# A fused attention and ResMLP kernel: LN1's beta as three PE rows, q by head groups and first-batch buffers in hT

## The chip, the cores and the metric

The kernel runs on one core of one Trainium2 chip. The metric is device microseconds (us) of a run. PE is the matmul engine, DVE the vector engine, ACT the scalar engine, and GpSimd (POOL in the views) is a further one; loads are issued by GpSimd, by SP and at the start by ACT. A transfer lands when all of its data has arrived; PE stands when it waits for something; the clock is the share of full speed that PE was granted. Most runs of a kernel agree within 0.3%. Medians are of 4 to 11 runs of the kernel before and 4 to 6 of the other. A ratio is the mean time of one kernel's fast runs over that of the other's of the same rounds, so it is not quite the ratio of the medians; it comes with a 95% interval.

## The reference, cut

```python
# q (8,16,384,64); k, v (8,4,384,64); four q heads share a k and v head
k = np.repeat(k, 4, axis=1); v = np.repeat(v, 4, axis=1)
scores = np.matmul(q, k.transpose(0, 1, 3, 2)) / np.sqrt(64)
attn = softmax(scores); attn_out = np.matmul(attn, v)
x = attn_out.transpose(0, 2, 1, 3).reshape(8, 384, 1024)
a1 = alpha1 * x + beta1                       # "LN1"
u = x + lam * np.einsum('ts,bsd->btd', w_tok, a1)   # token mix over 384 tokens
a2 = alpha2 * u + beta2
out = u + lam * (np.maximum(a2 @ w_ch1, 0.0) @ w_ch2)   # 1024 -> 4096 -> 1024
```

All tensors are f32 in HBM; the kernel computes in bf16 with f32 sums.

## The kernel before

For each of eight batches there is a side job (`side`: attention, token mix and transposes that end in `a2T`) and a main job (`main`: the MLP; the h matmuls with w1, then the ch matmuls with w2). The side job of batch b+1 is woven into the main job of batch b, and PE is full there. Only batch 0's side job stands alone, in front of everything: **the first stage**. The w1 matrix is streamed anew for every batch through a ring of five chunks (512 KB each as bf16), w2 is loaded once. GpSimd issues those loads, as it issues all loads that cast f32 to bf16.

The parts that the change touches, with cuts marked (`...`):

```python
            if hh == 0:
                avs[p] = psum.tile([P, 2, NST, D1], f32, tag="mm" if first else "av", name="av",
                                   bufs=2 if first else 1)
            av = avs[p]
            hk = (2 * p + hh) // G
            for sq in range(NST):
                for sk in range(NST):
                    k = (p * NST + sk) * NST + sq
                    nc.tensor.matmul(out=av[:, hh, sq, :], lhsT=ess[k // 4][:, hh, k % 4, :],
                                     rhs=vb[:, sk, hk, :], start=(sk == 0), stop=(sk == NST - 1))
            if hh == 0:
                if first and p in (0, 2):
                    r = slice(0, 256) if p == 0 else slice(256, DM)
                    nc.vector.tensor_tensor(out=g1[:, r], in0=g1[:, r], in1=lam_t[:, r], op=MUL)
                    nc.vector.tensor_tensor(out=h1[:, r], in0=h1[:, r], in1=lam_t[:, r], op=MUL)
                return
            rinv = sb.tile([P, 2, NST, 1], f32, tag="rinv", name="rinv", bufs=1)
            nc.vector.reciprocal(out=rinv, in_=av[:, :, :, D:])
            for hh in range(2):
                c0 = (2 * p + hh) * D
                nc.vector.tensor_tensor(out=x[:, :, c0:c0 + D], in0=av[:, hh, :, :D],
                                        in1=rinv[:, hh].to_broadcast([P, NST, D]), op=MUL)
            t = sb.tile([P, NST, P], f32, tag="tmp", name="a1f", bufs=4)
            nc.vector.tensor_tensor(out=t, in0=x[:, :, cols(p)], in1=bc(g1, p), op=MUL)
            a1s[p] = sb.tile([P, NST, P], bf, tag="a1", name="a1", bufs=2)
            eng = nc.gpsimd if first and p < NP - 2 else nc.vector
            eng.tensor_tensor(out=a1s[p], in0=t, in1=bc(h1, p), op=ADD)
        ...
        def tok(p):
            ps = psum.tile([P, NST, P], f32, tag="av" if first else "sc", name="tok",
                           bufs=1 if first else 2)
            for tt in range(NST):
                for st in range(NST):
                    nc.tensor.matmul(out=ps[:, tt, :], lhsT=wtokT[:, st, tt * P:(tt + 1) * P],
                                     rhs=a1s[p][:, st, :], start=(st == 0), stop=(st == NST - 1))
            u = x[:, :, cols(p)]
            nc.vector.tensor_tensor(out=u, in0=ps, in1=u, op=ADD)
            a2s[p] = sb.tile([P, NST, P], bf, tag="a2", name="a2", bufs=3)
            nc.vector.tensor_tensor(out=a2s[p], in0=u, in1=bc(al2, p), op=MUL)

        def a2_transpose(p):
            if not pe_flip or first and p < NP - 3:
                nc.sync.dma_start_transpose(
                    out=a2T[:, p, :S].rearrange("p (a s) -> p a s", a=NST),
                    in_=a2s[p].rearrange("p a d -> p (a d)"))
```

The prologue, in the order in which each engine meets its instructions, and the loads woven into the first stage (the key is the index of a step of `side(0)`):

```python
        nc.scalar.dma_start(out=qst, in_=q[0, :G].rearrange("h (p st) d -> p h st d", st=NST))
        load_q(0, [0], G)
        ...
        nc.gpsimd.tensor_copy(out=vt[0][:, :, :, :D], in_=vst.rearrange("p h st d -> p st h d"))
        place_k(0, 0)
        for h, cp in ((0, nc.vector.tensor_copy), (2, nc.scalar.copy)):
            cp(out=qrs[0][:, :, h:h + 2, :], in_=qst[:, h:h + 2].rearrange("p h st d -> p st h d"))
        load_k(1)
        for t, ap in ((g1, moe_alpha1), (lam_t, moe_lam), (h1, moe_beta1)):
            bcast(nc.scalar, t, ap, 0, 256)
            bcast(nc.sync, t, ap, 256, DM)
        bcast(nc.sync, al2, moe_alpha2, 0, DM)
        wtok_in = stage[:, 1, :NST * S // 2].bitcast(bf).rearrange("p (tt s) -> p tt s", tt=NST)
        ...
        for c in range(RING):
            load_w1(c)
        loads = {7: [(load_w2, 0, 0, 2)], 25: [(load_q, 1, [0]), (load_q, 1, [1])],
                 31: [(load_q, 1, [2]), (load_v, 1, [0])], 37: [(load_v, 1, [1])], 43: [(load_v, 1, [2])]}
        for i, f in enumerate(side(0)):
            f()
            for g, *a in loads.get(i, []):
                g(*a)
            if i == 4:
                place_k(0, 1)
```

In `main(0)` each chunk's end issues the chunk five further on, and for most chunks a piece of w2 as well. The first step of `side(1)` that needs q of batch 1 is its second, a transpose on PE, which comes after 32 h matmuls.

The softmax here doesn't subtract the row's maximum and nothing guards it: scores larger than these inputs give would overflow.

## Time and profile before

| | before |
|---|---|
| median of runs | 830.34 us (4 runs) |
| span of the profiled run | 828.8 us |
| first stage (to the first h matmul) | 52.04 us |
| a steady batch | 97 us, PE busy 96.40 |
| GpSimd's first w1 load | 8.67 us |
| last part of batch 1's q lands / PE wants it | 55.1 / 59.28 us |

The prediction below shows the lines that carry it. The two rows are the DMA view of the first 60 us in 40 slices of 1.5 us (busy share in tenths, then GB/s): the 16 DMA engines are busy from 3 to 57 us.

```profile
DMA  0599999999999999999999999899999999999208
GB/s 0 136 324 321 164 191 229 139 200 188 198 197 197 228 322 325 308 358 213 189 196 202 206 200 151 135 198 195 197 186 178 122 149 138 157 140 230 61 4 96
```

The view of waits between 20 and 52 us: who waited for what (total, times, longest). The same figure stood in a view that I had asked for before I predicted (waits from 0 to 52 us), but I did not weigh it, and it matters later: the DVE stood for the a2 buffer 1.0 us, although the chain of waits shows a DMA piece of 8.32.

```profile
DVE a L247 <- DMA a2T<-a: 1.0, 1, 1.0
```

### The profile page before, as it was taken

The page shows a single profiled execution, that of the slowest core. Times are in us where ns is not written, and L with a number is a line of the kernel's source. Part 1 is how long each engine was busy: PE and PEld are TensorE (multiplying, and loading weights), DVE is VectorE, ACT ScalarE, POOL GpSimd, SP SyncE. Part 2 cuts the span into 40 slices and gives each one's busy share as a digit, 9 for nine tenths or more (in the row PEclk, how much of TensorE's full clock was granted, in tenths as well). Part 3 has the DMA queues.
Part 4 walks back from the last instruction along what each step waited for, and adds up shares of the span by engine and source line. Part 5 has one row for each costly group of instructions (what it writes and reads, how often), then busy time and mean ns, then how long its engine had stood idle before and what let it go on. Part 6 is the DMA issues. An engine that isn't in the chain of part 4 may idle for free.

```text
span 828.8 us, 13904 instructions
## 1 busy us (share of the span) xinstructions
PE 797.1 (96%) x5958; PEld 445.9 (54%) x6011; DVE 350.9 (42%) x728; ACT 219.0 (26%) x287; POOL 187.6 (23%) x229
## 2 busy tenths in 40 slices
PE   5679999999999999999999999999999999999997
PEld 2456555566455654556555664556545565556543
DVE  3854645234452445434443344434444344442222
ACT  3514331233103321043211332133310342102100
POOL 5414441033302250022400224012410221003000
PEclk7869999999999999999999999999999999999999
DMA  9999999799948999499917999379995999119701
GB/s 193 230 145 181 200 210 190 138 175 151 140 97 134 176 169 90 97 166 173 169 46 138 181 169 138 82 128 179 174 91 111 130 176 141 37 55 182 97 38 39
DMA packets 265342, 115.09 MB, mean 139 GB/s; under 512 B 113728, under 2 KB 258496, under 8 KB 265280
## 3 DMA queue, kind: packets, MB, share of 16 engines
q0 software_dynamic: 200832, 83.28, 91.2%
q1 hardware_dynamic: 63488, 30.13, 15.6%
q10 hardware_dynamic: 960, 0.79, 0.4%
q8 instruction: 47, 0.77, 0.4%
q14 instruction: 15, 0.12, 0.0%
HBM read 172.56 MB, written 12.58 MB: 223 GB/s over the span
## 4 chain that ended last, share of the span: by engine, by line
PE 92%; DMA 3%; DVE 2%; issue 1%; ACT 1%; POOL 0%; SPq 0%; DVEq 0%; POOLq 0%
PE h L344 41%; PE ch L368 40%; PE av L217 4%; PE sc L188 4%; PE tok L242 4%; DMA q_raw<-in_q_dram 1%; DMA h<-in_moe_beta_dram 1%; DMA a2T<-a 1%; DVE a L247 1%; ACT hT L352 0%; DVE x L229 0%; DVE x L245 0%; DVE a1f L232 0%; PE tp L171 0%; PE tp L257 0%
## 5 line engine op out<-in xcount | busy, mean ns | idle before, releaser
L344 PE MATMUL h<-a2T,w 128*128 128x384 bf16 (+1 forms) x2048 | 356.6, 327 | 1.2 <-DVE bias L350 0.2
L368 PE MATMUL ch<-w,hT 128*128 128x512 bf16 x1483 | 345.1, 379 | 3.5 <-issue 1.1
L344 PEld LDWEIGHTS <-w 128*128 128x128 bf16 x2048 | 192.9, 98 | 129.4 <-issue 10.6
L127 POOL DMA_DIRECT2D w<-in_moe_w_ch_dram x128 | 112.3, 879 | 549.3 <-PE h L344 514.3
L368 PEld LDWEIGHTS <-hT 128*128 128x128 bf16 x1536 | 142.6, 98 | 155.6 <-issue 4.4
L194 ACT ACTIVATE es<-sc 128x1024 bf16<-128x1024 f32 x144 | 141.2, 1021 | 302.9 <-PE sc L188 302.9
L354 DVE TENSOR_SCALAR hT<-h,bias 128x384 bf16<-128x384 f32 x128 | 78.9, 617 | 186.1 <-PE h L344 185.5
L352 ACT ACTIVATE hT<-h,bias 128x384 bf16<-128x384 f32 x128 | 74.3, 581 | 229.6 <-PE h L344 202.6
L373 DVE TENSOR_TENSOR o<-ch,lam 128x512 f32<-128x512 f32 x48 | 33.0, 688 | 96.9 <-PE ch L368 96.9
L245 DVE TENSOR_TENSOR x<-tok,x 128x384 f32<-128x384 f32 x64 | 35.5, 555 | 82.9 <-PE tok L242 82.9
L217 PEld LDWEIGHTS <-es 128*128 128x128 bf16 x1152 | 52.4, 99 | 23.1 <-issue 1.6
L217 PE MATMUL av<-v,es 128*128 128x65 bf16 x1152 | 56.8, 196 | 0.8 <-ACT es L194 0.6
L242 PE MATMUL tok<-a,wtokT 128*128 128x128 bf16 x576 | 45.0, 226 | 8.8 <-DVE x L245 8.7
L242 PEld LDWEIGHTS <-wtokT 128*128 128x128 bf16 x576 | 38.9, 101 | 22.8 <-issue 6.5
L188 PE MATMUL sc<-qT,kT 64*128 64x384 bf16 (+2 forms) x576 | 46.5, 278 | 0.7 <-DVE qT L175 0.7
L229 DVE TENSOR_TENSOR x<-av,rinv 128x192 f32<-128x192 f32 x128 | 39.8, 352 | 2.3
L247 DVE TENSOR_TENSOR a<-x,al 128x384 bf16<-128x384 f32 x64 | 38.2, 597 | 3.2 <-DMA a2T<-a 1.0
L226 DVE RECIPROCAL rinv<-av 128x6 f32<-128x6 f32 x64 | 12.3, 192 | 59.5 <-PE av L217 59.3
L232 DVE TENSOR_TENSOR a1f<-x,g 128x384 f32<-128x384 f32 x64 | 36.0, 563 | 2.4
L188 PEld LDWEIGHTS <-kT 64*128 64x128 bf16 x576 | 20.1, 95 | 28.0 <-issue 23.6
L374 DVE TENSOR_TENSOR o<-o,x 128x512 f32<-128x512 f32 x48 | 33.2, 692 | 1.6
L235 DVE TENSOR_TENSOR a<-a1f,h 128x384 bf16<-128x384 f32 x58 | 32.5, 561 | 2.2
(38 smaller groups left out, 127.9 us busy)
## 6 DMA issues: line engine op xcount, KB each, us to landing
w<-in_moe_w_ch_dram POOLq DMA_DIRECT2D x135, 512.0 KB, 7.6
out_dram<-o SPq DMA_DIRECT2D x48, 256.0 KB, 2.2
q_raw<-in_q_dram POOLq DMA_DIRECT2D x21, 256.0 KB, 8.8
kst<-in_k_dram SPq DMA_DIRECT2D x16, 192.0 KB, 2.8
w<-in_moe_w_ch_dram POOLq DMA_DIRECT2D x10, 256.0 KB, 12.1
w<-in_moe_w_ch_dram POOLq DMA_DIRECT2D x1, 2048.0 KB, 35.0
v<-in_v_dram POOLq DMA_DIRECT2D x21, 64.0 KB, 8.8
a2T<-a SPq DMA_TRANSPOSE x53, 3.3
```

Of the source, the lines that this page charges most:

```text
L127: nc.gpsimd.dma_start(out=t, in_=w1src[:, :, c * CW * P:(c + 1) * CW * P])
L188: nc.tensor.matmul(out=sc[:, hh, k % 4:k % 4 + n], lhsT=kT[r, sk, 2 * p // G, :], rhs=qT[r, st:st + n, p, :], start=True, stop=True)
L194: nc.scalar.activation(out=e, in_=sc, func=EXP, scale=scale_qk)
L217: nc.tensor.matmul(out=av[:, hh, sq, :], lhsT=ess[k // 4][:, hh, k % 4, :], rhs=vb[:, sk, hk, :], start=(sk == 0), stop=(sk == NST - 1))
L229: nc.vector.tensor_tensor(out=x[:, :, c0:c0 + D], in0=av[:, hh, :, :D], in1=rinv[:, hh].to_broadcast([P, NST, D]), op=MUL)
L232: nc.vector.tensor_tensor(out=t, in0=x[:, :, cols(p)], in1=bc(g1, p), op=MUL)
L242: nc.tensor.matmul(out=ps[:, tt, :], lhsT=wtokT[:, st, tt * P:(tt + 1) * P], rhs=a1s[p][:, st, :], start=(st == 0), stop=(st == NST - 1))
L247: nc.vector.tensor_tensor(out=a2s[p], in0=u, in1=bc(al2, p), op=MUL)
L344: nc.tensor.matmul(out=ps[:, :n], lhsT=w1[:, dt, j * P:(j + 1) * P], rhs=a2T[:, dt, :n], start=(dt == 0), stop=(dt == NDT - 1))
L352: nc.scalar.activation(out=hT[:, nt, :], in_=ps[:, :S], func=RELU, bias=c1)
L354: nc.vector.tensor_scalar(out=hT[:, nt, :], in0=ps[:, :S], scalar1=c1, scalar2=0.0, op0=ADD, op1=mybir.AluOpType.max)
L368: nc.tensor.matmul(out=ps, lhsT=hT[:, nt, ms * P:(ms + 1) * P], rhs=w2[:, nt, cs], start=(nt == 0), stop=(nt == NNT - 1))
```

## The change

Its intent is to shorten the first stage. LN1's beta is no longer added on DVE or GpSimd: the token mix gets a further matmul whose three rows hold beta and the row sums of w_tok in bf16 parts. The q of batch 0 comes in four groups of heads, in order of need, the later three by way of a staging area inside the x tile. The exp results, a1 and a2 of batch 0 lie in hT (the tile for the hidden values of the MLP), which is idle then, with more places than before. Products and copies are spread anew: alpha1 x lam and the placing of q groups 2 and 3 go to GpSimd, ahead of its w1 loads.

```diff
             def exp():
-                e = sb.tile([P, 2, 4, P], bf, tag="es", name="es", bufs=EB)
+                if first:
+                    e = hTf[:, i % 6 * 1024:(i % 6 + 1) * 1024].rearrange("p (h k s) -> p h k s", h=2, k=4)
+                else:
+                    e = sb.tile([P, 2, 4, P], bf, tag="es", name="es", bufs=EB)
                 nc.scalar.activation(out=e, in_=sc, func=EXP, scale=scale_qk)
        ...
+            if first:
+                a1s[p] = hTf[:, 6144 + p % 3 * S:6144 + (p % 3 + 1) * S].rearrange("p (a d) -> p a d", a=NST)
+                nc.vector.tensor_tensor(out=a1s[p], in0=x[:, :, cols(p)], in1=bc(g1, p), op=MUL)
+                return
             t = sb.tile([P, NST, P], f32, tag="tmp", name="a1f", bufs=4)
             nc.vector.tensor_tensor(out=t, in0=x[:, :, cols(p)], in1=bc(g1, p), op=MUL)
             a1s[p] = sb.tile([P, NST, P], bf, tag="a1", name="a1", bufs=2)
-            eng = nc.gpsimd if first and p < NP - 2 else nc.vector
-            eng.tensor_tensor(out=a1s[p], in0=t, in1=bc(h1, p), op=ADD)
+            nc.vector.tensor_tensor(out=a1s[p], in0=t, in1=bc(h1, p), op=ADD)
        ...
-                                     rhs=a1s[p][:, st, :], start=(st == 0), stop=(st == NST - 1))
+                                     rhs=a1s[p][:, st, :], start=(st == 0),
+                                     stop=(st == NST - 1 and not first))
+                if first:
+                    nc.tensor.matmul(out=ps[:, tt, :], lhsT=R[:, tt * P:(tt + 1) * P],
+                                     rhs=H[:, cols(p)], start=False, stop=True)
             u = x[:, :, cols(p)]
             nc.vector.tensor_tensor(out=u, in0=ps, in1=u, op=ADD)
-            a2s[p] = sb.tile([P, NST, P], bf, tag="a2", name="a2", bufs=3)
+            if first:
+                a2s[p] = hTf[:, 7296 + p % 5 * S:7296 + (p % 5 + 1) * S].rearrange("p (a d) -> p a d", a=NST)
+            else:
+                a2s[p] = sb.tile([P, NST, P], bf, tag="a2", name="a2", bufs=3)
        ...
+        def three_rows(out, t, full, m):
+            nc.vector.tensor_copy(out=t, in_=full)
+            nc.vector.scalar_tensor_tensor(out=out, in0=t, scalar=eye3[:, m:m + 1], in1=full,
+                                           op0=MUL, op1=mybir.AluOpType.subtract)
+
+        def rows_h():
+            be = rows[:, :DM]
+            nc.vector.tensor_tensor(out=be, in0=be, in1=h1[:3], op=MUL)
+            three_rows(H, rows[:, DM:DM + DM // 2].bitcast(bf), be, 2)
+
+        def rows_r():
+            ps = psum.tile([P, S], f32, tag="av", name="r", bufs=1)
             for st in range(NST):
-                ps = tp_ps([P, NST, P])
-                for tt in range(NST):
-                    nc.tensor.matmul(out=ps[:, tt, :], lhsT=wv[:, tt, st, :], rhs=ident,
-                                     is_transpose=True, start=(tt == 0),
-                                     stop=(tt == NST - 1), skip_group_check=True)
-                nc.vector.tensor_copy(out=wtokT[:, st, :], in_=ps.rearrange("p a b -> p (a b)"))
+                nc.tensor.matmul(out=ps[:3], lhsT=ones3, rhs=wtokT[:, st, :], start=(st == 0),
+                                 stop=(st == NST - 1))
+            three_rows(R, rows[:, DM:DM + S // 2].bitcast(bf), ps[:3], 1)
```

and the prologue:

```diff
+        qhs = {g: xs[0][:, g - 1, 512:].bitcast(bf)[:, :G * NST * D].rearrange("p (h st d) -> p h st d", h=G, st=NST)
+               for g in (1, 2, 3)}
        ...
+        load_q4(1)
         make_identity(nc, ident)
+        nc.gpsimd.dma_start(out=wtok_in, in_=moe_w_tok.rearrange("(p tt) s -> p tt s", tt=NST))
+        load_q4(2)
+        load_q4(3)
        ...
         nc.gpsimd.tensor_copy(out=vt[0][:, :, :, :D], in_=vst.rearrange("p h st d -> p st h d"))
+        for lo, hi in ((0, 256), (256, DM)):
+            for t, ap in ((g1, moe_alpha1), (lam_t, moe_lam), (al2, moe_alpha2)):
+                bcast(nc.sync, t, ap, lo, hi)
+            nc.gpsimd.tensor_tensor(out=g1[:, lo:hi], in0=g1[:, lo:hi], in1=lam_t[:, lo:hi], op=MUL)
         place_k(0, 0)
        ...
+        place_q4(2, nc.gpsimd)
+        place_k(0, 1)
+        place_q4(3, nc.gpsimd)
+        for c in range(RING - 1):
             load_w1(c)
-        loads = {7: [(load_w2, 0, 0, 2)], 25: [(load_q, 1, [0]), (load_q, 1, [1])],
-                 31: [(load_q, 1, [2]), (load_v, 1, [0])], 37: [(load_v, 1, [1])], 43: [(load_v, 1, [2])]}
+
+        def late_loads():
+            load_k(1)
+            with nc.allow_non_contiguous_dma(reason="one small vector, once"):
+                nc.sync.dma_start(out=be2, in_=moe_beta2.rearrange("(dt di) -> di dt", di=P))
+            bcast(nc.sync, h1, moe_beta1, 0, DM)
+
+        loads = {9: [(load_w1, RING - 1), (load_w2, 0, 0, 2)], 20: [(late_loads,)], 30: [(load_q, 1)], 37: [(load_v, 1)]}
```

## The prediction

> **What bounds the kernel now.** I read the page first. Its table of engines has PE busy for 797.1 of 828.8 us, and its slices show where the rest is: only at the start.
>
> ```profile
> PE   5679999999999999999999999999999999999997
> PEclk7869999999999999999999999999999999999999
> ```
>
> Each digit is a tenth of a 20.7 us slice. From the fourth slice on PE is full at full clock. A cut of the span into stages gives sizes (busy us of each engine, then granted clock, DMA share, GB/s):
>
> ```profile
> 0.00:52.20 52.20, 30.07 (x352) 20.08 (x353) 31.65 (x73) 21.09 (x23) 22.37 (x29) 0.74 1.49 201
> 52.20:148.00 95.80, 94.83 (x754) 53.97 (x758) 48.17 (x120) 30.80 (x44) 34.30 (x43) 0.98 1.37 186
> 148.00:245.00 97.00, 96.40 (x719) 53.41 (x724) 39.65 (x80) 26.31 (x34) 21.46 (x26) 1.00 1.10 140
> ```
>
> The steady batches (third row) lose 0.6 us in 97, so a change to the first batch can gain only in the first 52.2 us, where no engine is full (DVE, the busiest, 31.65 us). The chain of waits over this stretch names what holds it (start, length, what):
>
> ```profile
> 3.98 10.29 DMA q_raw<-in_q_dram
> ...
> 17.61 9.60 DMA h<-in_moe_beta_dram
> ...
> 37.87 8.32 DMA a2T<-a
> ```
>
> Three DMA waits: the rest of the first q, LN1's beta (DVE stands before the product with lam, in order), and a DMA transpose that keeps one of three a2 buffers. Between them DVE runs through its per-head-pair work. The first MLP matmul (h, L344) follows at 52.04. The change goes for all three.
>
> Then I asked what the DMA engines do meanwhile. In a view of DMA up to 60 us their busy digit is 9 from 3 to about 57 us: the backlog of w1 (5 chunks), half of w2, the vectors, and q and v of batch 1. Issues in two windows (16 to 60, size, median us from issue to landing) and PE just after the stage:
>
> ```profile
> w<-in_moe_w_ch_dram POOLq DMA_DIRECT2D x1, 2048.0 KB, 35.0
> q_raw<-in_q_dram POOLq DMA_DIRECT2D x1, 256.0 KB, 17.5
> ...
> q_raw<-in_q_dram POOLq DMA_DIRECT2D x1, 256.0 KB, 17.8
> ```
>
> ```profile
> 52.04 5.77 PE L344 MATMUL h<-a2T,w 128*128 128x385 bf16 x24
> 57.64 0.50 PE L162 MATMUL tp<-ident,k 128*128 128x128 bf16 x6
> 57.98 1.47 PE L344 MATMUL h<-a2T,w 128*128 128x385 bf16 x8
> 59.28 0.50 PE L171 MATMUL tp<-ident,q_raw 128*128 128x128 bf16 x6
> ```
>
> The half of w2, issued at 13.0, lands at 48.0. Batch 1's q comes in three parts behind it: the first, issued at 34.05, lands at 51.5; the last, issued at 37.33, at 55.1. PE's queue meets the first transpose of that q at 59.28, 7.2 us after the MLP began. It needs all three parts. So there are **only 4.2 us of slack** behind the stage that the change shortens. This is what I rest the prediction on.
>
> **What the Trainium skill says.** (1) "DMA: Bandwidth & Descriptors", section Issuing engines are not separate DMA queues: transfers begun from any engine share the same 16 DMA engines. The trace agrees: a w1 chunk takes about 2.6 us alone (landings at 28.9, 31.6, 34.2), but between 21.9 and 28.9, beside the four vectors on SP's queue, one took 7 us. Spreading loads over queues buys no throughput. (2) "TensorE: Matmul & The Clock Gate", Part 1: after an idle window of about 3.4 us the clock is halved until activity has lasted about as long. It agrees: the clock reads 0.50 from 8 to 16 and again around 44 to 55 us, and the first 24 h matmuls take 5.56 us of the chain where 24 later take 3.92, so a cold start costs 1.6 us. (3) "SBUF — State Buffer", Who interferes with whom: a DVE instruction with two SBUF inputs contends with a GpSimd one that reads SBUF. It agrees: L247 takes 0.56 us alone but 1.07 to 1.39 us while GpSimd does the beta addition (L235, 1.00 us each). (4) "VectorE: DVE Perf Modes", TRN2 errata: a ScalarE copy out of PSUM costs 172 cycles plus one per element at 1.2 GHz. For 128x384 this is 463 ns; the trace has 479. I use it for 128x768: 783 ns.
>
> **The change, part by part.**
> Beta as three PE rows. DVE loses the products with lam (L222 and L223: 0.41 + 0.42 + 0.96 + 0.96 = 2.75 us) and two additions (1.1), GpSimd six of 1.00; L247 falls from 6.9 us to 8 x 0.56 = 4.5 (2.4 saved). PE gains 24 row matmuls: nine tok matmuls take 0.68 us warm, so three more cost 0.2 a pair, 1.6 in all, beside DVE. Building the rows costs DVE an estimated 4.1: three passes over 1024 elements on three partitions (128x768 took 0.96, so two products of 1.23 and a cast of 0.7) and two over 384 (0.5 each).
> Q by groups. The slow first load (three of 12 heads in 256 B rows, landing up to 14.3) becomes four heads at a time in 768 B rows, then a copy into place. The 10.3 us wait should go. DVE gets one placing copy (0.4) and 0.15 for the split evacuation; two evacuations of q and one of k (1.65) and two casts of k (0.74) leave it. ACT takes the three evacuations, 3 x 0.78 = 2.3 us.
> Buffers in hT. Exp results get 6 places, a1 three, a2 five instead of three: the 8.3 us wait for a transpose to free a2 goes.
> DVE in this stage: 31.65 - 2.75 - 1.1 - 2.4 - 1.65 - 0.74 + 4.1 + 0.4 + 0.15 = 27.7 us. It starts on k at 4.1, so it can't end before 32; the tail (transpose, copy) and small stalls put **the first h matmul at 38 (35 to 42), 14 us earlier**. ACT needs 18 exps at 0.97 from about 6.8 plus 2.3, ending near 27, so it isn't the bound.
>
> **What the earlier start meets.** Little of the DMA work ahead of batch 1's q is removed: w1 x5, half of w2, k of batch 1 and the vectors are all still in front of it. Before, from 14.2 to 55.1 this was 41 us: w1 and w2 (9.4 MB read as f32, twice what lands, at 400 GB/s by the 2.6 us a chunk) 23.6, vectors and k 5.5, token weights 1, five transposes 3.5 (w2 took 13.8 us where 10.4 would do), q itself 7. After, the vectors needed first and the token weights come before; from w1's start there remain 23.6 + 3.5 + 6.7 + 2.5 (beta's late load, k) = 36.3. When does w1 start? GpSimd now has, before the first w1, to wait for v (0.83 copy), lam's and alpha's long parts (which I put at 13 us: some 4.5 MB at about 350 GB/s, the rate in the slices of the DMA view where the vectors moved), multiply them (128x384 takes 1.00, so 768 about 1.9), copy two q groups (0.9 each) and cast k twice (0.55): 13 + 1.9 + 1.8 + 1.1 = 18 against 8.67 before. First bytes at 18.5; 1.5 of the 2.5 hide in the gap. So batch 1's q lands at 18.5 + 36.3 - 1.5 = **53.3**, only about 2 us sooner. PE would reach its transpose at 38 + 7 = 45, and stand some 8 us. The gain at this instruction: 59.3 - 53.3 = 6.0, less a cold restart of up to 1.6 after so long a stand: 4.4. Behind it the MLP needs as long as before. **830.2 - 4.4 = 825.8 us.**
>
> **Rivals.**
> A. The full gain: if q of batch 1 comes in time, 14 us, about 816. For it: the loads of q and v move up in the program. Against: they are on the same GpSimd queue, behind w1 and w2, where the landings above come in order of issue.
> B. The stage itself stays long (45 us or more), since the GpSimd chain delays q's second half or DVE meets new waits. It changes nothing as long as the h matmuls begin before 46: the DMA wait covers it.
> C. The w1 stream of the MLP of batch 0 becomes the next bound. From 64 to 100 us the queue moves 200 GB/s and landings grow from 5.8 to 14.2 us, so it lags; chunk 15, issued near 86, lands near 99, needed near 103. Starting 14 us sooner with the same bytes would exceed this slack; 4 to 6 us sooner does not, as about 4 us in which the DMA engines stand nearly idle (57 to 61) are filled. Second half of w2: last landing 129.3, first output tile of that half starts at 133.4 and reaches it 7 us later; safe. A full-gain start would lose some here: about 820.
> D. Nothing gained or slightly slower (830 to 832), if GpSimd's w1 loads come even later than 20 us.
>
> **Range and chances.** The first w1 load may be at 14 to 21 us, which moves q's landing between 49 and 57 and the time between 821 and 830; better DMA use early would add 1 to 2 us. I take 819.5 to 830. A gain of 2% needs under 813.6, that is a start at 36 or sooner and no DMA wait at all: 4%. Slower by 2%: 1%.
>
> **What would show it.** Right: h at 35 to 42; no wait of several us for beta or for an a2 buffer; L247 at 0.56; first w1 load on GpSimd at 15 to 20; PE waiting several us on q_raw in batch 1's first transpose, at half clock after it. Wrong: no such wait, or the time lost in h matmuls waiting on w (rival C), or a stage that ends after 45 (B). What would upset me most is the order of landings: if q does not queue behind w2 as the trace suggests, A holds.

## The result

| | before | changed |
|---|---|---|
| median | 830.34 us (829.16 to 830.49) | 834.65 us (833.53 to 836.85) |
| ratio | | 1.0058, 95% interval 1.0035 to 1.0081 |
| span of the profiled run | 828.8 | 835.0 |
| first h matmul | 52.04 | 52.81 |
| GpSimd's first w1 load | 8.67 | 23.20 |
| PE's first transposes of batch 1's q done by | 59.8 | 65.0 |

So the change made the kernel 0.6% slower; it had been forecast 0.5% faster. The interval leaves out 1. What follows takes as long as before: from the end of the eight h matmuls behind that transpose (61.1 and 67.5 us) to the end of the span it is 767.7 us before and 767.5 after. The profiled run of the changed kernel was the slowest of its four (836.85), so its trace shows a loss of 6.2 us, of which the medians show 4.3.

PE around the end of the first stage (start, length, instructions, idle time before them and what ended it). These lines answer to the four of PE in the prediction:

```profile
52.81 6.21 PE L375 MATMUL h<-a2T,w 128*128 128x385 bf16 x24
...
59.19 1.47 PE L375 MATMUL h<-a2T,w 128*128 128x385 bf16 x8
60.62 0.23 PE L177 MATMUL tp<-ident,q_raw 128*128 128x128 bf16 x1
62.52 0.23 PE L177 MATMUL tp<-ident,q_raw 128*128 128x128 bf16 x1 [1.67 <-DMA q_raw<-in_q_dram]
64.36 0.61 PE L177 MATMUL tp<-ident,q_raw 128*128 128x128 bf16 x4 [1.61 <-DMA q_raw<-in_q_dram]
64.76 2.75 PE L375 MATMUL h<-a2T,w 128*128 128x385 bf16 x8
```

The stand for batch 1's q is there, part by part as the three loads land, and the eight h matmuls after it take 2.75 us instead of 1.47; the granted clock over them was 0.53. The time before the transposes' end has grown by 5.2 us, and the cold clock adds 1.3.

Why does q land at 64.3? GpSimd's own row of the timeline shows when the stream in front of it began, first in the kernel before, then in the changed one:

```profile
8.67 4.40 POOL L127 DMA_DIRECT2D w<-in_moe_w_ch_dram  x5
```

```profile
10.21 0.83 POOL L460 CAST v<-stage 128x768 bf16<-128x768 f32 x1 [5.27 <-DMA stage<-in_v_dram]
13.22 1.57 POOL L464 TENSOR_TENSOR g<-g,lam 128x256 f32<-128x256 f32 x1 [2.19 <-DMA lam<-in_moe_lam_dram]
18.68 1.80 POOL L464 TENSOR_TENSOR g<-g,lam 128x768 f32<-128x768 f32 x1 [3.89 <-DMA lam<-in_moe_lam_dram]
20.43 0.82 POOL L448 COPY q_raw<-x 128x768 bf16<-128x768 bf16 x1
...
23.20 4.47 POOL L129 DMA_DIRECT2D w<-in_moe_w_ch_dram  x5
```

The w1 loads stand in GpSimd's queue behind products that wait for lam. The chain of waits shows SP's issue of lam's long part at 8.58 and its landing at 18.55:

```profile
8.58 9.97 DMA lam<-in_moe_lam_dram
```

While it waits and then computes, the DMA engines run dry. This is the row of stages for 18 to 23 us (busy us of PE, PEld, DVE, ACT, GpSimd; then granted clock, DMA share, GB/s), with a DMA share of 0.06 where it was 1.31 before:

```profile
18.00:23.00 5.00, 0.12 (x2) 0.12 (x2) 1.68 (x5) 0.00 (x0) 4.32 (x5) 0.50 0.06 20
```

And why is the first stage no shorter? DVE's row shows a wait that the change brought:

```profile
14.14 0.18 DVE L230 RECIPROCAL rinv<-av 128x6 f32<-128x6 f32 x1
21.28 0.62 DVE L233 TENSOR_TENSOR x<-av,rinv 128x192 f32<-128x192 f32 x2 [6.97 <-POOL q_raw L448]
```

DVE may not write x while GpSimd has yet to copy a q group out of the same tile. The two regions don't overlap, but seen as ranges of addresses they do: the write takes columns 0 to 63 of each of x's three planes, and the staged groups 1 and 2 lie in columns 512 and up of the first and second. Group 3 lies in the third, beyond the end of that range, and the wait did end with the copy of group 2 (20.43 + 0.82 = 21.25), not with that of group 3 (22.10 + 1.15 = 23.25).

### The profile page after: what moved, and what is told of

Its sections match the earlier page's. It is cut to its first block, busy times and chain, and to the rows that moved or that the text cites. A ratio compares the mean times of both kernels' runs of the same rounds, so it can differ in the third digit from the quotient of the medians.

```text
span 835.0 us, 14036 instructions
## 1 busy us (share of the span) xinstructions
PE 806.4 (97%) x6044; PEld 446.8 (54%) x6044; DVE 350.3 (42%) x724; ACT 221.1 (26%) x290; POOL 190.2 (23%) x232
## 4 chain that ended last, share of the span: by engine, by line
PE 92%; DMA 5%; DVE 1%; ACT 1%; POOL 1%; SPq 0%; issue 0%; ACTq 0%; POOLq 0%
PE ch L399 40%; PE h L375 40%; PE av L225 4%; PE sc L193 4%; PE tok L249 4%; DMA q_raw<-in_q_dram 3%; DMA lam<-in_moe_lam_dram 1%; SPq L119 0%; DMA stage<-in_q_dram 0%; ACT hT L383 0%; POOL q_raw L107 0%; DVE x L233 0%; POOL g L464 0%; PE tp L177 0%; PE tp L271 0%
## 5 line engine op out<-in xcount | busy, mean ns | idle before, releaser
L399 PE MATMUL ch<-w,hT 128*128 128x512 bf16 x1536 | 353.2, 379 | 0.0
L202 ACT ACTIVATE es<-sc 128x1024 bf16<-128x1024 f32 x126 | 123.4, 1021 | 284.9 <-PE sc L193 284.9
L225 PEld LDWEIGHTS <-es 128*128 128x128 bf16 x1008 | 45.8, 97 | 20.5
L225 PE MATMUL av<-v,es 128*128 128x65 bf16 x1008 | 49.0, 193 | 0.0
L193 PE MATMUL sc<-qT,kT 64*128 64x384 bf16 (+2 forms) x576 | 45.2, 273 | 0.3 <-ACT hT L202 0.3
L249 PE MATMUL tok<-a,wtokT 128*128 128x128 bf16 x504 | 37.3, 219 | 0.1
L261 DVE TENSOR_TENSOR a<-x,al 128x384 bf16<-128x384 f32 x56 | 31.4, 561 | 1.9
L240 DVE TENSOR_TENSOR a1f<-x,g 128x384 f32<-128x384 f32 x56 | 31.2, 558 | 1.9
## 6 DMA issues: line engine op xcount, KB each, us to landing
w<-in_moe_w_ch_dram POOLq DMA_DIRECT2D x1, 2048.0 KB, 29.8
```

What stands on the lines that cost most here:

```text
L193: nc.tensor.matmul(out=sc[:, hh, k % 4:k % 4 + n], lhsT=kT[r, sk, 2 * p // G, :], rhs=qT[r, st:st + n, p, :], start=True, stop=True)
L202: nc.scalar.activation(out=e, in_=sc, func=EXP, scale=scale_qk)
L399: nc.tensor.matmul(out=ps, lhsT=hT[:, nt, ms * P:(ms + 1) * P], rhs=w2[:, nt, cs], start=(nt == 0), stop=(nt == NNT - 1))
```

## The experiments

Two theories. **D**: the time is set by when batch 1's q lands, that by the DMA stream in front of it, and that by when GpSimd starts it. **S**: the length of the first stage sets the time, and the false wait on x is the loss. A third, **C**, comes from the prediction: once q is in time, the w1 chunks behind it are the bound. Twelve runs of eleven kernels followed (best1 ran twice), all with correct results; h is the first h matmul, q the end of PE's stand for batch 1's q (or the time it met that q without a stand, marked -).

| kernel | first w1 load | h | q | median | ratio to before, 95% interval |
|---|---|---|---|---|---|
| before | 8.67 | 52.04 | 59.28 - | 830.34 | |
| changed | 23.20 | 52.81 | 64.36 | 834.65 | 1.0058 (1.0035 to 1.0081) |
| a_stage | 22.34 | 46.90 | 62.39 | 835.96 | 1.0069 (1.0052 to 1.0086) |
| b_order | 21.48 | 52.04 | 59.64 - | 832.93 | 1.0024 (1.0007 to 1.0040) |
| ab_both | 22.46 | 45.13 | 53.38 - | 831.56 | 1.0013 (0.9998 to 1.0028) |
| c_before_late | 22.65 | 49.12 | 61.33 | 835.20 | 1.0060 (1.0041 to 1.0078) |
| g_bufs | 8.22 | 50.45 | 57.51 - | 829.64 | 1.0002 (0.9987 to 1.0017) |
| e_early | 4.89 | 47.38 | 57.16 | 830.42 | 1.0016 (0.9998 to 1.0035) |
| f_pace | 22.69 | 43.60 | 53.71 | 830.30 | 1.0006 (0.9979 to 1.0032) |
| best1 | 13.54 | 45.22 | 52.37 - | 825.41 | 0.9954 (0.9931 to 0.9976) |
| p_before | 8.61 | 51.73 | 59.28 - | 831.45 | 1.0015 (0.9993 to 1.0037) |
| best1_again | 11.47 | 45.64 | 52.81 - | 825.88 | 0.9942 (0.9926 to 0.9959) |
| k128 | 11.90 | 41.80 | 50.15 - | 822.93 | 0.9912 (0.9894 to 0.9929) |
| best2 | 12.90 | 42.75 | 48.31 - | 823.35 | 0.9913 (0.9885 to 0.9942) |

### a_stage: the changed kernel without the false wait

```diff
-        qhs = {g: xs[0][:, g - 1, 512:].bitcast(bf)[:, :G * NST * D].rearrange(...)
+        qhs = {g: w2[:, NNT - g, :G * NST * D].rearrange(...)      # loaded much later
```

> The changed kernel, but the three staged q groups lie in a corner of w2 that is loaded much later, not in the x tile, so that DVE's first write of x no longer waits 7.0 us for GpSimd's copy out of it. Theory D (the time is set by when batch 1's q lands, and that by when GpSimd starts the w1 stream at 23.2): the first h matmul comes at 44 to 48 instead of 52.8, q still lands at 63 to 66, PE stands 10 us or more before its first transpose, time within 1.5 of 834.6. Rival S (the length of the first stage sets the time): the time falls as the stage does, to 826 to 830.

The compiled program's first write of x lost just the two waits that were meant (the one on GpSimd, for the copy of group 2, and one on the load into the staging area):

```
-L233 TensorTensor x<-av,rinv 128x3x64 [waits DMASW2_49,DVE_49,Pool_49]
+L233 TensorTensor x<-av,rinv 128x3x64 [waits DVE_49]
```

PE's rows at the end of the stage:

```profile
46.90 6.32 PE L375 MATMUL h<-a2T,w 128*128 128x385 bf16 x24
...
58.79 0.29 PE L177 MATMUL tp<-ident,q_raw 128*128 128x128 bf16 x1 [3.93 <-DMA q_raw<-in_q_dram]
60.62 0.29 PE L177 MATMUL tp<-ident,q_raw 128*128 128x128 bf16 x1 [1.54 <-DMA q_raw<-in_q_dram]
62.39 0.61 PE L177 MATMUL tp<-ident,q_raw 128*128 128x128 bf16 x4 [1.49 <-DMA q_raw<-in_q_dram]
```

The stage is 5.9 us shorter and nothing is gained: PE only stands longer (7.0 us instead of 3.3). q landed 2 us sooner than in the changed kernel's trace, a little before the range that D gave; the first w1 load was 0.9 sooner too. The median of 835.96 is within 1.5 of 834.6 as D said. S is out.

### c_before_late: the kernel before with a late w1 stream

```diff
-        for c in range(RING):
-            load_w1(c)
-        loads = {7: [(load_w2, 0, 0, 2)], 25: ...
+        loads = {14: [(load_w1, c) for c in range(RING)] + [(load_w2, 0, 0, 2)], 25: ...
```

> The kernel before, with its w1 loads and half of w2 moved on GpSimd from 8.7 to about 23 us, as late as the changed kernel has them. Theory D: batch 1's q lands at 61 to 64 instead of 55.1, PE stands for it, and the kernel before becomes as slow as the changed one, 833 to 836, although its first stage gets shorter because beta lands sooner. Rival S: time the same or lower than 830.3.

```profile
49.12 5.95 PE L344 MATMUL h<-a2T,w 128*128 128x385 bf16 x24
...
61.33 0.61 PE L171 MATMUL tp<-ident,q_raw 128*128 128x128 bf16 x4 [1.35 <-DMA q_raw<-in_q_dram]
```

With none of the change in it but the late start of the stream, the kernel before becomes as slow as the changed one (835.20), with a first stage 2.9 us shorter; PE stood 4.1 us for q, as in the changed kernel part by part. This is the cause of the loss, produced by itself.

### e_early: a_stage with the stream started early

```diff
         nc.gpsimd.tensor_copy(out=eye3, in_=ident[:3, :3])
+        for c in range(RING - 1):
+            load_w1(c)
 ...
         place_q4(3, nc.gpsimd)
-        for c in range(RING - 1):
-            load_w1(c)
```

> a_stage with the first four w1 loads issued by GpSimd at about 5 us, before it waits for v and lam, so that the DMA engines no longer stand idle from 18 to 23 us. Theory D: q of batch 1 lands 4 to 6 us sooner than in a_stage, 57 to 59, lam and so the stage come later (h at 48 to 53), time 829 to 832. If the start of the w1 stream doesn't matter: 835 to 836 as a_stage.

```profile
57.16 0.40 PE L177 MATMUL tp<-ident,q_raw 128*128 128x128 bf16 x4 [1.42 <-DMA q_raw<-in_q_dram]
```

The opposite test: one edit on top of a_stage, and the time falls from 835.96 to 830.42 although the stage gets 0.5 us longer (these two ran on two chips, each beside the kernel before: ratios 1.0069 and 1.0016, intervals apart). q lands in the range given, 5 us sooner. Only the first four w1 loads started 17 us sooner: they filled the gap from 18 to 23 us (DMA share 1.43). The fifth and half of w2 still stood behind the products and were issued at 23.60 and 24.54; w2 came at 26.75 in a_stage, so only 2.2 us sooner. That, and the sharing of the DMA engines with the vectors, I take for the reason that no more came of it; it was not tested.

### b_order and ab_both: q ahead of w2

```diff
-        loads = {9: [(load_w1, RING - 1), (load_w2, 0, 0, 2)], ... 37: [(load_v, 1)]}
+        loads = {9: [(load_w1, RING - 1)], ... 37: [(load_v, 1), (load_w2, 0, 0, 2)]}
```

> The changed kernel, but half of w2 is loaded behind q and v of batch 1 instead of ahead of them. Theory D: q lands near 54 to 56, before PE wants it at 60.6, the stand of about 3.7 and the cold restart of 1.3 go: 829 to 830, or 830 to 832 if the w1 chunks behind w2 now come late. Rival S: the stage is the same, the time stays at 834.6 within 1.

> Both edits of a_stage and b_order. Theory D: h starts at 44 to 48, q lands at 54 to 56, wanted at 52 to 55, so 823 to 828. Rival S: as a_stage alone, 826 to 830 for both, no difference between the two.

In b_order PE no longer stands for q, and the median falls by 1.7 us, less than expected. In the profiled run the span was 829.0, just that of the kernel before; the three timed runs had spans near 831.2 and left no trace, so where the 2 us went in them stays open. In ab_both the stage ends at 45.13 and q is in time; but the gain is given back at a new place:

```profile
67.26 2.43 PE L375 MATMUL h<-a2T,w 128*128 128x385 bf16 x8 [3.68 <-DMA w<-in_moe_w_ch_dram]
```

The first w1 chunk behind w2 is late. In all, PE's h matmuls wait 5.0 us for w1 there, where they waited for none in b_order. That is C: of the 7 us by which the stage is shorter than in b_order, 1.4 remain.

### f_pace: w2 in pieces

```diff
-        loads = {... 37: [(load_v, 1), (load_w2, 0, 0, 2)]}
+        loads = {... 37: [(load_v, 1), (load_w2, 0, 0, 16), (load_w2, 0, 1, 16)]}
 # in main(0), after chunk c:
-            if b == 0 and 2 <= c < 12:
-                load_w2(*((0, 6 + c, 16) if c < 10 else (1, c - 10, 16)))
+            if b == 0:
+                for _ in range({0: 1, 2: 1, 4: 1, 6: 1, 8: 1, 9: 3, 10: 6}.get(c, 0)):
+                    load_w2(0, next(w2_pieces), 16)      # 2 .. 15
+                if c == 11: load_w2(1, 0, 16); load_w2(1, 1, 16)
```

> ab_both with the first half of w2 no longer as one 2 MB load behind q and v but in sixteen pieces, two there and the others spread over the MLP of batch 0, most of them after its last w1 load. Theory: in ab_both the wait for q was replaced by 5 us of waits of h matmuls for w1 chunks queued behind w2 (67.26); with the pieces spread they go, and the time is set by the stage: 824 to 827. If those waits are not the cause: 831.5 as ab_both.

The waits for w1 are gone, as expected; the time is not what was expected (830.30). PE stands 2.6 us for q of batch 1 after all, since h starts at 43.60 now, and a wait of another kind appears in the next batch:

```profile
PE sc L193 <- DMA qT<-q_raw: 2.8, 1, 2.8
```

q of batch 2 is transposed by DMA, and that transpose was issued at 150.04 (146.68 in ab_both). I take it that pushing w2 back pushed this q back; no run isolates it. The wait has moved a third time.

### g_bufs: one part of the change alone

The kernel before, with `es`, `a1` and `a2` of batch 0 in hT as in the change (its diff above); all else as before.

> The kernel before with one part of the change alone: exp results, a1 and a2 of the first batch in hT (6, 3 and 5 places). Theory D: the 8.3 us wait for a transpose goes, the first h matmul comes near 44 to 46, q of batch 1 still lands at 54 to 56, PE now stands 2 to 4 us for it, and only the old slack of 4.2 is gained, less the cold clock after it: 825.5 to 828. Rival S (stage length sets the time): the whole 7 to 8 us, 822 to 823.5.

A miss. The stage got 1.6 us shorter, not 8, and the timed runs show no gain (ratio 1.0002; the interval leaves room for 1.1 us). So the 8.3 us piece in the chain of waits was not 8.3 us of standing. It is the time from the transpose's issue to its landing, and DVE did useful work for most of it; the view of waits says 1.0. In both kernels DVE has its head-pair work nearly back to back from 28 to 50 us, and moving one wait inside a queue that is full does not end the queue sooner.

### best1, best1_again, p_before: the order and the stage together

best1 is f_pace with the queues reordered:

```diff
 GpSimd:  q group 1, identity, w_tok, [wait v] copy v,
-         (q groups 2 and 3 before v) ... both products, q2, k, q3, w1 x4
+         q groups 2 and 3, w1 x2, short product, copy q2, cast k, w1 x2, long product, copy q3
 SP:      k, v,
-         g lo, lam lo, al lo, g hi, lam hi, al hi
+         g lo, lam lo, g hi, lam hi, al
-        nc.gpsimd.tensor_tensor(out=h1, in0=h1, in1=lam_t, op=MUL)      # at the end of the stage
+        (the same, after the third step of side(1))
```

> f_pace with GpSimd's and SP's queues reordered (v before the later q groups, two w1 loads before the waits for lam, lam before alpha2, copies before the long product) and the late product of beta and lam moved off the end of the stage. Theory D: DMA idle gap gone, q of batch 1 lands at 44 to 50, h at 39 to 44, no wait for q or w above 1 us: 816 to 822. If the stage or the stream is bound elsewhere: 823 or more.

> best1 once more, for a comparison on one chip: 824 to 827, ratio 0.994 to 0.997.

> The kernel before with only the order of loads of f_pace and best1: q and v of batch 1 ahead of w2, w2's first half in sixteen pieces. If what best1 gains comes from the order of loads alone, 825 to 827. Theory D says that with the old stage (h at 52) q was in time anyway, so the order gains nothing by itself: 829 to 831.

best1 is faster than both kernels, 825.4 and 825.9, though less than I hoped; the stage ends at 45.2 instead of 39 to 44. No wait of PE for q or w above 0.2 us was left in best1 (1.9 us for the transposed q of batch 2 in the second profile). The same order of loads on the kernel before gives nothing (p_before, 831.45): with the old stage q was in time anyway. Neither the shorter stage (a_stage) nor the better order of loads (p_before) pays alone, and no gain of the two together is shown by f_pace (1.0006). best1 changes the order in two queues and the place of one product at once; which of these paid is not shown.

### k128 and best2: the cost of the three rows

In best1 the chain of waits of the stage consists of PE work for most of 20 to 44 us. There the three-row matmuls showed up. PE's rows for one head pair in best1_again:

```profile
33.56 0.34 PE L249 MATMUL tok<-hT,wtokT 128*128 128x128 bf16 x3
33.84 0.23 PE L253 MATMUL tok<-stage 3*128 3x128 bf16 x1
33.99 0.34 PE L249 MATMUL tok<-hT,wtokT 128*128 128x128 bf16 x3
...
34.70 0.22 PE L253 MATMUL tok<-stage 3*128 3x128 bf16 x1
```

From start to start three plain ones and a three-row one take 0.43 us; the kernel before took 0.68 for nine plain ones. k128 makes the row matmul a full one, with 125 rows of zeros:

```diff
-        R = stage[:3, 2120:2312].bitcast(bf); H = stage[:3, 2312:2824].bitcast(bf)
+        R = stage[:, 2120:2312].bitcast(bf); H = stage[:, 2312:2824].bitcast(bf)
+        nc.gpsimd.memset(stage[:, 2120:2824], 0.0)
-        three_rows(H, ...); three_rows(R, ...)
+        three_rows(H[:3], ...); three_rows(R[:3], ...)
```

> best1 with the row matmul of the token mix over all 128 partitions (rows 3 to 127 zero) in place of three. In best1 the three row matmuls of a pair take PE about 0.7 us instead of the 0.2 I had put for them. If that is the change of row group: three tok groups of 4 come to 0.85 to 0.95 us instead of 1.3 and the stage ends 2 to 4 us sooner, time 822 to 824. If it is the extra matmul as such, or PE isn't the path: no difference to best1.

```profile
31.84 0.34 PE L249 MATMUL tok<-hT,wtokT 128*128 128x128 bf16 x3
32.02 0.22 PE L253 MATMUL tok<-stage 128*128 128x128 bf16 x1
32.07 0.33 PE L249 MATMUL tok<-hT,wtokT 128*128 128x128 bf16 x3
```

The period is 0.23 us instead of 0.43: three periods a pair and eight pairs make 4.8 us of PE time, and the stage ends 3.8 us sooner than in best1_again on the same chip. Not all of it is the rows. One DVE product, 0.56 us alone, was held up beside GpSimd's long product and lay on the chain of waits in both, for 3.72 us in best1_again and for less in k128:

```profile
20.96 2.81 DVE L261 TENSOR_TENSOR hT<-x,al 128x384 bf16<-128x384 f32 x1
```

That is 0.9 of the 3.8. The last group of best1_again also ran at half clock (a period of 0.64 instead of 0.43, some 0.6 us). So 2.3 to 2.9 are left for the rows. The time falls from 825.88 to 822.93; the two intervals against the kernel before overlap by a hair (0.9926 and 0.9929). best2 also builds the rows earlier and drops three warm-up matmuls:

```diff
-        at = {1: [(warmup, 3)], 2: [(warmup, 3), (place_q4, 1, ...), (q_transpose, 2, ...), (rows_h,)],
+        at = {1: [(rows_h,), (warmup, 3)], 2: [(place_q4, 1, ...), (q_transpose, 2, ...)],
```

> k128 with DVE's passes that build the beta rows put in front of the second group of q, where DVE stands idle for 3 us, and three warm-up matmuls fewer. Expected: first reciprocal at 13 instead of 15.7, stage 1 to 3 us shorter than k128, time 820 to 823 unless q of batch 1, landing near 47 to 50, becomes the bound again (then as k128).

The first reciprocal came at 13.41 as expected, but the stage ended at 42.75, not sooner than in k128 (a DVE product was held up 3.83 us this time), and its runs spread from 819.5 to 826.6. Inconclusive; k128 is the version that I would keep.

## Why the prediction was wrong, point by point

**Slack behind the stage: right.** The step "only 4.2 us of slack", with batch 1's q queued behind w1 and w2, is where the time was decided. Loads landed in order of issue, and PE stood at that transpose (3.3 us) and ran cold after it (1.3). a_stage, c_before_late and e_early show it from three sides. The reading of the clock beside it was incomplete: before the change it read 0.50 also from 32 to 38 us, and it fell near 7.8 us, before any gap in PE's rows had passed 1.6 us, so that stretch doesn't bear out the 3.4 us of idle that the prediction cites. The cold start of 1.6 us was measured and holds.

**The step that failed: "First bytes at 18.5", and so "53.3".** GpSimd issued its first w1 load at 23.20, outside the 14 to 21 that I allowed. The term that was mis-sized is the arrival of lam's long part, put at 13; it landed at 18.55, and GpSimd's product began at 18.68. The 13 came from 4.5 MB at 350 GB/s; from 3 to 18.55 us the DMA engines moved 232 GB/s. The other terms held: the long product 1.80 (1.9), the copies 0.82 and 1.15 (0.9 each). Of the 11.1 us between 53.3 and 64.36, 5.2 come from here (23.20 against 18.0).

**The rest of that sum was too small as well.** From the first w1 load to q's landing I had 35.3 us (0.5 to the first bytes, then 34.8); it took 41.1. Half of w2, issued at 27.6, landed 29.8 us later, at 57.4; q itself took 6.9, as I had it. 1.5 us are explained: k of batch 1 and beta were to hide in the gap, but SP issued the second half of k and beta only from 22.1 on, since k's buffer came free with GpSimd's casts. The remaining 4 or so are not settled.

**The stage, "38 (35 to 42)": wrong by 14.8.** The sum of DVE's work was not far off (27.7 us; it was busy 30.09 up to 52.81), and the estimate of 783 ns for ACT's larger copies measured 0.79 to 0.82. What failed is the step from "DVE has 27.7 us of work" to an end at 38: DVE did not run through. The largest part is the false wait on x, which I had not seen in the diff: 5.9 us by a_stage. The four kernels that lack it and keep the order of the early queues in the main ended the stage anywhere from 43.60 to 47.38, so one profile each leaves that figure uncertain by some 2 us either way. The three rows are the next part: "0.2 a pair" in my sum, and 0.68 in the trace (1.36 from the first start to the last end in best1_again, less 0.68); k128, without that cost, ended the stage 3.8 us sooner than its neighbour on the same chip, of which 2.3 to 2.9 are the rows' part. The new order of queues in best1 shows no shortening beyond that scatter. Of the 3.8 us from k128's 41.80 to my 38, the held-up DVE product explains up to 2.25 (2.81 less 0.56): the change took GpSimd's beta additions away from DVE's side, but set longer products there (1.99 us for the same product at the end of the changed kernel's stage). The rest is not explained. The length of the stage did not matter for the time of the changed kernel: a_stage and the changed kernel take the same.

**The waits that go.** I counted 8.3 us for the a2 buffer from the chain of waits. By g_bufs it was worth 1.6. The 9.6 us for beta is such a piece too: DVE stood 2.3 us for lam and 0.3 for beta around it.

**Rival D** of the prediction is what came: "if GpSimd's w1 loads come even later than 20 us". I gave 830 to 832; it was 834.65, because they came later still. **Rival B** came too (a stage of over 45 us, from a new wait of DVE and the GpSimd chain), and at 52.81 it was past the 46 up to which I had called it harmless; a_stage shows that it cost nothing all the same, since q's landing covered it. **Rival C** was real but hidden behind the q wait; it appeared as soon as q was moved forward (ab_both, 5.0 us).

## What to carry to other kernels

Before shortening a stage, find the first transfer that the next stage needs, its slack, and which instruction starts the stream in front of it; here 4.2 us of slack bounded a 14 us plan. Don't let loads that feed a long stream stand in an engine's queue behind arithmetic that waits for another load. And a DMA piece in a chain of waits is a latency, not standing time: the view of waits tells how long the engine stood.

## What the Trainium skill lacked or had wrong

- "TensorE: Matmul & The Clock Gate", section LDWEIGHTS: it says that a weight load's time is set by the columns, not by K. The load itself agrees (0.09 us for three rows, 0.10 for 128), but a three-row matmul between 128-row ones stretched the group of four from 0.23 to 0.43 us, and zero-padding it to 128 rows removed that. "TensorEngine Tiling (Array Packing)", Key Properties, says that a change of tiling mode drains the engine, which may be this cost; neither page gives its size, and no run here separates the switch from the three rows themselves.
- "DMA: Bandwidth & Descriptors", section Issuing engines are not separate DMA queues: true here, but it calls the issue time usually small beside the transfer. What decided here was when the issuing engine reached the issue: loads behind GpSimd's waits left the DMA share at 0.06 for 5 us. SP's issues of vectors, 0.42 to 0.46 us each in the kernel before, took 1.3 to 2.1 us each between 4.8 and 12 us of the changed kernel.
- "SBUF — State Buffer", section Who interferes with whom: agrees, with times that it doesn't have. A DVE instruction of 0.56 us with two SBUF inputs took 1.99 us beside one GpSimd product of 2.36 us in the changed kernel, 2.73 us in a_stage and 3.83 in best2. In all three it ended 0.42 to 0.43 us after GpSimd's product, whenever it had begun.
- No page says that a wait can come from two regions of a tile that interleave without overlapping; DVE stood 6.97 us for it here. It is a matter of the program's tracking of tiles and not of the chip.
